# Gated FNet and PEER mix on one core: operand sums moved into DRAM transfers, row transposes moved to DMA

## The chip, the cores and the metric

The kernel runs on one core of a Trainium2 chip. The metric is device time in microseconds (us), the median of several runs. Five engines work side by side, each on its own list of instructions in order: TensorE (PE) multiplies matrices, VectorE (DVE), ScalarE (ACT) and GpSimd (POOL) work on elements, and SyncE (SP) mostly issues DMA transfers. ACT and POOL can issue transfers too. An instruction that waits holds up all that stands behind it on its engine.

## The reference

The input x has 2048 rows of 640 numbers. Two branches are computed from it and mixed row by row with a gate.

```python
g = sigmoid((x * gate_w).sum(-1))
# branch A: a Fourier transform over both axes, real part, as matrix products
a = einsum("sd,ed->se", x, dft_hid_re);  b = einsum("sd,ed->se", x, dft_hid_im)
y = dft_seq_re @ a - dft_seq_im @ b
# branch B: 32 heads; each scores 16 + 16 keys and takes the best two of each,
# then the best two of the four sums (of 256 experts); softmax over those two
act = gelu(einsum("nd,nhkd->nhk", x, u[top_e]))
o = einsum("nhk,nhk,nhkd->nd", softmax(top_s), act, v[top_e])
return g * y + (1 - g) * o
```

## The kernel before

Every matrix product in float32 is made of three products: each operand is split into a high part (an ACT copy to fp32r) and a low part (a subtraction on POOL or DVE); `split` does that and `mm3` issues the three matmuls. `mm3` and `split` are helpers, so nearly all matmuls carry the lines L127 to L129 and all splits L122 (ACT) and L123 (POOL or DVE).

**First stage, 128 pieces.** `seq_piece(n)` multiplies x by one 128 x 512 block of the sequence transform: two matrices (`w`), four column blocks of 512 (`c`), 16 pieces each, 15 matmuls in a piece. Piece n loads the block of piece n + 5 (tile `wf`, five buffers, on SP's queue) and splits that of piece n + 3 into one of the four slots of `WS`. After the 16 pieces of a block its five sums are evicted to `ST`, multiplied by the gate on DVE (`gate_piece`, L192) and stored to DRAM as `pd[w, c]` (`store_piece`, L201, issued by ACT).

What else is to be done is hung behind pieces: `at(n, f)` puts f into the program behind piece n. Up to piece 31 the key matrix is prepared, from piece 31 to 71 (`N0` to `N1`) score products for branch B are put between the pieces, from 71 on the hidden transform's matrices are loaded and split (`load_dd`, `split_dd`, tiles with the tags `xf`, `xh`, `xl`).

**The pump.** DVE's work for branch B is a list of small steps that `Pump` puts into the program between PE's matmuls. Each matmul group adds its time to a credit (times `share`: 0.95, or 1.05 while the experts run), each step takes its cost off, and other DVE work takes off its own (`bg.credit -= ...`). `topk` picks the best keys of a tile of 128 rows, `gates` makes the weights of four tiles, and `rows` turns the results so that heads lie on partitions: six PE transposes in one group for two tiles into a PSUM bank, two ACT copies (L501) from there into `ROWS`. `bg.space(f, us)` calls f when that much matmul time has gone by since the step before it.

When all 16 tiles have rows, `experts` starts: 32 chunks (2 halves of 16). For each, DVE builds one-hot tiles (`hot`, three operations, cost 3.3), PE multiplies them (16 matmuls, L593), DVE sums the result into `cd` (L579, L581, cost 1.4). From piece 120 on (`ending`) there is one chunk at a time.

**Second stage, 70 steps.** The hidden transform is done on blocks of 2 x 2 with seven products in place of eight, for two pairs `b` of column blocks, 35 steps each (`step(m)`). The operands are four blocks of the pair (`a11`, `a12`, `a21`, `a22`, that is `pd[0]` and `pd[1]` of the pair's two columns) or sums of them:

- s3 = a21 + a11, s1 = a21 + a22, s2 = s1 + a11, s4 = s2 + a12.

The order of the products is a11, a12, s1, s2, s4, s3, a22, five steps each. `load_a` loads an operand block of 256 KB on SP's queue into a buffer given out by `take` and given back by `give`; `split_step` splits it five steps ahead. The sums come about in two ways. For the pair b = 0, `load_parts` loads the blocks behind pieces 95 to 106, `sum_parts` adds them on DVE and `store_parts` stores the four sums to DRAM (`pq`). For b = 1, blocks are loaded again and added in place on DVE at steps 39 to 52 (`add_a`).

At the start of each half, `load_z` brings in the branch B operands: it drains the pump until the half's sums `cd` are issued, stores them (`gd`, L549), loads them back (L806) with the activations (`actd`) and the gate, and `split_z` multiplies them on DVE (L819, L820) and splits them into `zo`.

Of the kernel before, what the change touches and what calls it, by code (L numbers as in the profile page):

```python
# [8 lines left out]
F32 = mybir.dt.float32  # L9
F32R = mybir.dt.float32r  # L10
F16 = mybir.dt.float16
AF = mybir.ActivationFunctionType
OP = mybir.AluOpType
# [3 lines left out]
P = 128  # L17
# [7 lines left out]
NT = S // P  # L25
NP = NT // 2
TC = 512
NC = S // TC
NPC = 2 * NC * NT
KD = D // P  # L30
HALF = D // 2
NG = HH // 8
NB = 4
# [57 lines left out]
def gated_mix_kernel(ctx: ExitStack, tc: tile.TileContext, xT, xn, dreT, dimT, wsre, wsim, wq, kT, uT, vv, gw, out):  # L91
    nc = tc.nc
# [3 lines left out]
    big = ctx.enter_context(tc.tile_pool(name="big", bufs=1))  # L96
    dram = ctx.enter_context(tc.tile_pool(name="dram", bufs=1, space=bass.MemoryType.DRAM))
# [8 lines left out]
    def bank(n, shape=(P, TC), dt=F32):  # L106
        return psum.tile(list(shape), dt, name=f"b{n}", tag=f"b{n}")
# [4 lines left out]
    def ps_t(shape, dt=F32):  # L112
        return bank(7, shape, dt)
# [6 lines left out]
    def split(f, h, l, eng):  # L120

        nc.scalar.activation(h, f, AF.Copy)  # L122
        eng.tensor_sub(l, f, h.bitcast(F32))  # L123
# [5 lines left out]
        nc.tensor.matmul(o, wl, ah, start=False, stop=last, skip_group_check=more)  # L129

    pd = {(w, c): dram.tile([KD, P, TC], F32, name=f"pd{w}{c}", tag=f"pd{w}{c}") for w in range(2) for c in range(NC)}
    pq = {u: dram.tile([KD, P, TC], F32, name=f"pq{u}", tag=f"pq{u}") for u in ("s1", "s2", "s4", "s3")}
    actd = dram.tile([2, P, S], F32, name="actd")
    gd = [dram.tile([2, 4, E, E, P], F32, name=f"gd{g}", tag=f"gd{g}") for g in range(2)]
    gdr = dram.tile([S], F32, name="gdr")
    bg = Pump()
# [16 lines left out]
    pf, psp, X, xr = {}, {}, {}, {}  # L153
# [17 lines left out]
    def at(n, f, *args):  # L171
        then.setdefault(n, []).append(lambda: f(*args))
# [5 lines left out]

    banks = []
    p3, last_part, ending, share = None, False, False, 0.95  # L180
    grow, staged, P22 = {}, {}, {}

    def load_row(q):
        grow[q] = pools[-1].tile([P, TC], F32, name="grow", tag="grow")
# [10 lines left out]

    def store_piece(q):
        w, c = divmod(q, NC)
        if q == NC + 1:
            P22.update((d, staged[q, d]) for d in range(KD))
        for d in range(KD):  # L200
            nc.scalar.dma_start(pd[w, c][d], staged.pop((q, d)))  # L201

# [20 lines left out]
    for q in range(2 * NC):  # L223
        n = NT * (q + 1)
        at(n + (2 if q == 0 else -2 if q > 1 else -1), load_row, q)
        at(n + (7 if q == 0 else 0), gate_piece, q)
        at(n + (8 if q == 0 else 1), store_piece, q)
# [47 lines left out]
    t = ps_t([P, 512])  # L275
# [18 lines left out]
    ident = const.tile([P, P], F16)  # L294
# [52 lines left out]
    xf, xs = {}, {}  # L347
# [25 lines left out]
    n = bursts[-1]  # L373
# [28 lines left out]
    ROWS = [cp.tile([P, 3, P, 8], F16, name=f"rows{g}") for g in range(2)]  # L402
    p2_stack = ctx.enter_context(ExitStack())
    p2 = p2_stack.enter_context(tc.tile_pool(name="p2", bufs=1, reuse_waits="tile"))
# [5 lines left out]
    picked, rowed = set(), set()  # L410
# [79 lines left out]
    def rows(b):  # L490
        rp, gs = gated.pop(b)

        def row_tiles(a):
            t = ps_t([P, 2, 3, P], F16)
            for m in range(2):
                for n in range(2):
                    nc.tensor.transpose(t[:, m, n, :], rp[:, n, a + m].rearrange("p a k h -> p (a k h)"), ident)  # L497
                nc.tensor.transpose(t[:, m, 2, :], gs[:, a + m].rearrange("p a k h -> p (a k h)"), ident)
            for m in range(2):
                i = b * NB + a + m  # L500
                nc.scalar.activation(ROWS[i // 8][:, :, :, i % 8], t[:, m], AF.Copy)  # L501
                rowed.add(i)

        for a in range(0, NB, 2):
            bg.space(lambda a=a: row_tiles(a), 7.0 if a else 20.0 if b == NT // NB - 1 else 12.0)
        yield 0.0

    def done(i, gen):
# [3 lines left out]
    def picks(i, sc):  # L512
        bg.add(done(i, topk(i, sc)))
        if i % NB == NB - 1:
            bg.add(gates(i // NB))
        elif i and i % NB == 0:
            bg.add(rows(i // NB - 1))
        if i == NT - 1:
            bg.add(rows(NT // NB - 1))
# [14 lines left out]
    for p in range(NP):  # L534
        n = N0 + 5 * p
# [4 lines left out]
    N1 = N0 + 5 * NP  # L540
# [174 lines left out]
    at(NPC + 28, store_gates, 1)  # L715


    raw_free, raw_tags = deque(), [("wf", 1)] * 5 + [(f"X{s}", 2) for s in range(10, 16)] + [("xf", 2)]
    raw, sp = {}, {}

    def take(key):
        if raw_tags:
            t, n = raw_tags.pop(0)
            if t == "wf":
                raw_free.append(big.tile([P, TC], F32, name="ra", tag=t, bufs=5))
            else:
                r = big.tile([P, 2, TC], F32, name="ra", tag=t)
                raw_free.extend(r[:, a] for a in range(2))
        raw[key] = f = raw_free.popleft()
        return f  # L730

    def give(key):
        raw_free.append(raw.pop(key))

    def load_a(b, what, k, row, col):
        f = take((b, what, k))
        nc.sync.dma_start(f, pd[col - 1, 2 * b + row - 1][k] if row else pq[what][k])

    def add_a(b, o, what, k, last):
        nc.vector.tensor_add(raw[b, o, k], raw[b, o, k], raw[b, what, k])  # L740
        bg.credit -= 0.75
        if last:
            give((b, what, k))


    PS, parts = [], {}

    def load_parts(k):

        if not PS:  # L750
            PS.extend(big.tile([P, 2, TC], F32, name="ps", tag=t) for t in ("xf", "xh", "xl"))
        parts[k] = [t[:, k % 2] for t in PS]
        for f, q in zip(parts[k], ((0, 1), (0, 0), (1, 0))):
            nc.sync.dma_start(f, pd[q][k])

    def sum_parts(k, n):
        f21, f11, f12 = parts[k]
        f22 = P22[k]
        if n == 0:
            nc.vector.tensor_add(f22, f22, f21)  # L760
            nc.vector.tensor_add(f21, f21, f11)
        else:
            nc.vector.tensor_add(f11, f11, f22)
            nc.vector.tensor_add(f12, f12, f11)
        bg.credit -= 1.5

    def store_parts(k, n):
        f21, f11, f12 = parts[k]
        for u, f in (("s2", f11), ("s4", f12)) if n else (("s1", P22[k]), ("s3", f21)):
            nc.sync.dma_start(pq[u][k], f)  # L770

    for k, (n, m) in enumerate(((-1, 2), (0, 4), (5, 7), (7, 9), (10, 12))):
        n, m = NT * (NC + 2) + n, NT * (NC + 2) + m
        at(n, load_parts, k)
        for a in range(2):
            at(m + a, sum_parts, k, a)
            at(m + 2 + a, store_parts, k, a)

    def ring(m):
        return WP[:, m % 6] if m % 6 < 2 else WS[:, m % 6 - 2]  # L780

    def split_step(m):
        if m < 2 * NSTEP:
            b, (u, k) = m // NSTEP, divmod(m % NSTEP, KD)
            what = UNITS[u]
            key = (b, "s" if b and what in ("s1", "s2", "s4") else what, k)
            sp[m] = ring(m)[:, 0], ring(m)[:, 1]
            split(raw[key], *sp[m], nc.vector if what in ("s2", "s3") else nc.gpsimd)
            bg.credit -= 0.8 if what in ("s2", "s3") else 0.0
            if b == 0 or what in ("a11", "a12", "a22", "s3", "s4"):  # L790
                give(key)

    zop = {}

    def load_z(b, n):

        c = 2 * b + n
        bg.drain(lambda: b in summed)
        store_gates(b)
        nc.sync.dma_start(take((b, "g", n)), gdr[c * TC:(c + 1) * TC].partition_broadcast(P))  # L800
        for k in range(2):
            a, f = take((b, "za", k)), take((b, "zf", k))
            nc.sync.dma_start(a, actd[k][:, c * TC:(c + 1) * TC])
            for i in range(4):
                i8 = (4 * c + i) % 8
                nc.sync.dma_start(f[:, i * P:(i + 1) * P],  # L806
                                  gd[b][i8 // 4, i8 % 4].rearrange("e f m -> (e f) m")[k * P:(k + 1) * P])
# [74 lines left out]
    def step(m):  # L882
        b, (u, k) = m // NSTEP, divmod(m % NSTEP, KD)
        what = UNITS[u]
        if k == 0:
# [8 lines left out]
            if what == "a22":  # L894
                z_group("Z", 0, v_neg, first=True)
        split_step(m + AHEAD)
        o, w, w5 = {
            "a11": ("X", lambda a: DD[:, 0, a, k, 0:2 * P], lambda a: DD[:, 0, a, k, 4 * P:]),
# [51 lines left out]
    M = NPC  # L950
# [8 lines left out]
    M = NPC + NSTEP  # L959
    for k in range(KD):  # L960
        at(M - 8 + k, load_a, 1, "a11", k, 1, 1)
        at(M - 4 + k, load_a, 1, "a12", k, 1, 2)
        at(M + k, load_a, 1, "s", k, 2, 2)
        at(M + k, load_a, 1, "s3", k, 2, 1)
        at(M + 4 + k, add_a, 1, "s", "s3", k, False)
        at(M + 5 + k, load_a, 1, "a11", k, 1, 1)
        at(M + 8 + k, add_a, 1, "s", "a11", k, False)
        at(M + 8 + k, add_a, 1, "s3", "a11", k, True)
        at(M + 8 + k, load_a, 1, "a12", k, 1, 2)
        at(M + 13 + k, add_a, 1, "s", "a12", k, True)  # L970
        at(M + 21 + k, load_a, 1, "a22", k, 2, 2)
    for b in range(2):
        M = NPC + b * NSTEP
        for n, i in ((0, -1), (1, 21)):
# [76 lines left out]
```

## Time and profile before

| | |
|---|---|
| three runs | 787.89, 788.63, 789.27 us; median 788.63 |
| the profiled execution | 788.78 us, its span 787.0 us |
| busy share of the span | PE 99%, weight loads 79%, DVE 70%, POOL 43%, ACT 35% |
| matmuls | 4164 |
| DMA | 128.73 MB, mean 164 GB/s |
| granted PE clock | 0.998 |

The profile is of one execution. The span runs from the first to the last instruction on the core. In a row of groups, the number behind x is the count, then come the busy time and the mean of one in ns, then the idle time of the engine just before them and what ended it. In a timeline row, the start and the length in us stand first. In a row of waits: in total, how often, the longest. Matmuls are pipelined and their ends are modelled, so the pace is read from start to start.

### The profile page before, as it was taken

How to read it: one execution, taken by the hardware profiler on the slowest of the kernel's cores; microseconds unless marked ns; L12 is line 12 of the kernel's file. 1: busy time of each engine (PE TensorE's matmuls, PEld its weight loads, DVE VectorE, ACT ScalarE, POOL GpSimd, SP SyncE). 2: the span in 40 equal slices, each digit the busy share in tenths (PEclk: the TensorE clock that was granted, in tenths of full speed). 3: DMA queues.
4: the chain of work that ended last, by engine and by line, in shares of the span. 5: the costliest groups of instructions: out<-in, count | busy, mean ns of one | idle time of the engine just before them, and what ended most of it. 6: DMA issues, size and time to landing. Idle time of an engine off the chain costs nothing.

```text
span 787.0 us, 11023 instructions
## 1 busy us (share of the span) xinstructions
PE 777.9 (99%) x4164; PEld 625.3 (79%) x4164; DVE 550.5 (70%) x660; ACT 274.3 (35%) x445; POOL 335.1 (43%) x233
## 2 busy tenths in 40 slices
PE   9999999999999999999999999999999999998997
PEld 6777677888888888888888888888888877777886
DVE  6741022286887799499969598899989947673861
ACT  5344323321316332532353551311334344323350
POOL 5423224315334241533415784444346573355370
PEclk9999999999999999999999999999999999999999
DMA  9966995403022230305213533578855795329621
GB/s 347 370 246 189 322 342 183 166 13 101 20 96 86 108 114 14 100 14 186 77 60 121 189 121 104 164 234 266 266 167 172 255 314 173 108 64 305 216 84 67
DMA packets 67828, 128.73 MB, mean 164 GB/s; under 512 B 9408, under 2 KB 16448, under 8 KB 67520
## 3 DMA queue, kind: packets, MB, share of 16 engines
q1 hardware_dynamic: 55024, 110.60, 42.2%
q10 hardware_dynamic: 12752, 17.45, 6.2%
q8 instruction: 32, 0.52, 0.3%
q14 instruction: 20, 0.16, 0.1%
HBM read 102.84 MB, written 25.17 MB: 163 GB/s over the span
## 4 chain that ended last, share of the span: by engine, by line
PE 92%; DMA 3%; POOL 1%; issue 1%; SPq 1%; ACT 1%; DVE 0%; ACTq 0%; DVEq 0%; POOLq 0%
PE b L127 30%; PE b L128 29%; PE b L129 29%; PE b L320 2%; DMA ra<-pqs 1%; PE b L593 1%; DMA ra<-actd 1%; POOL WS L123 1%; PE b L332 1%; PE b L213 1%; POOL zo L123 1%; DMA ra<-gd 0%; DMA wf<-in_wsre 0%; SPq L806 0%; PE b L497 0%
## 5 line engine op out<-in xcount | busy, mean ns | idle before, releaser
L123 POOL TENSOR_TENSOR WS<-wf,WS 128x512 fp32r<-128x512 f32 x127 | 190.0, 1502 | 272.7 <-ACT WS L122 254.8
L127 PE MATMUL b<-WS,X 128*128 128x512 f32 x635 | 251.3, 396 | 0.1
L129 PE MATMUL b<-WS,X 128*128 128x512 f32 x635 | 247.6, 390 | 0.0
L128 PE MATMUL b<-WS,X 128*128 128x512 f32 x635 | 247.5, 390 | 0.0
L127 PEld LDWEIGHTS b<-WS,X 128*128 128x128 f32 x635 | 119.2, 188 | 32.8 <-issue 7.8
L129 PEld LDWEIGHTS b<-WS,X 128*128 128x128 f32 x635 | 119.2, 188 | 25.4
L128 PEld LDWEIGHTS b<-WS,X 128*128 128x128 f32 x635 | 119.3, 188 | 24.0 <-POOL WS L123 0.4
L122 ACT ACTIVATE WS<-wf 128x512 fp32r<-128x512 f32 x128 | 80.1, 629 | 128.5 <-PE b L129 75.5
L437 DVE TENSOR_REDUCE mm<-sc 128x64 f32<-128x1024 f32 x32 | 39.0, 1219 | 45.2 <-ACT sc L423 44.7
L123 POOL TENSOR_TENSOR xl<-xf,xh 128x640 fp32r<-128x640 f32 x16 | 33.0, 2086 | 73.4 <-ACT xh L122 73.4
L127 PE MATMUL b<-WU,xh 128*128 128x512 f32 x160 | 62.7, 392 | 0.0
L129 PE MATMUL b<-WU,xl 128*128 128x512 f32 x160 | 62.3, 389 | 0.0
L128 PE MATMUL b<-WU,xh 128*128 128x512 f32 x160 | 62.3, 389 | 0.0
L423 ACT ACTIVATE sc<-b 128x512 f32<-128x512 f32 x32 | 20.5, 641 | 114.4 <-PE b L129 114.4
L123 POOL TENSOR_TENSOR WS<-ra,WS 128x512 fp32r<-128x512 f32 x32 | 45.6, 1444 | 27.8 <-ACT WS L122 27.8
L192 DVE SCALAR_TENSOR_TENSOR ST<-ST,grow 128x512 f32<-128x512 f32 x40 | 35.7, 956 | 18.3 <-DMA grow<-gdr 18.3
L335 DVE TENSOR_TENSOR WU<-b,WU 128x512 fp32r<-128x512 f32 (+1 forms) x16 | 7.8, 490 | 57.3 <-ACT WU L334 57.3
L439 DVE TENSOR_TENSOR eq<-sc,mm 128x1024 f16<-128x1024 f32 x32 | 45.5, 1423 | 1.1
L579 DVE TENSOR_TENSOR tmp<-b,mask 128x512 f32<-128x512 f32 x32 | 22.0, 689 | 30.4 <-PE b L593 29.3
L443 DVE TENSOR_REDUCE rr<-eq 128x64 f16<-128x1024 f16 x32 | 39.0, 1220 | 1.1
L123 POOL TENSOR_TENSOR WP<-ra,WP 128x512 fp32r<-128x512 f32 x18 | 26.8, 1498 | 29.5 <-ACT WP L122 29.4
L122 ACT ACTIVATE WS<-ra 128x512 fp32r<-128x512 f32 x46 | 28.0, 627 | 25.5 <-PE b L129 14.4
(152 smaller groups left out, 1258.1 us busy)
## 6 DMA issues: line engine op xcount, KB each, us to landing
wq<-in_wq SPq DMA_DIRECT2D x32, 640.0 KB, 6.5
wf<-in_wsre SPq DMA_DIRECT2D x64, 256.0 KB, 5.5
wf<-in_wsim SPq DMA_DIRECT2D x64, 256.0 KB, 3.8
ra<-pd SPq DMA_DIRECT2D x50, 256.0 KB, 4.1
pd<-ST ACTq DMA_DIRECT2D x40, 256.0 KB, 3.0
xr<-in_xn SPq DMA_DIRECT2D x16, 320.0 KB, 5.9
xf<-in_xT SPq DMA_DIRECT2D x16, 320.0 KB, 3.3
ra<-pqs SPq DMA_DIRECT2D x20, 256.0 KB, 4.3
```

The costliest lines, as they stand in the source:

```text
L122: nc.scalar.activation(h, f, AF.Copy)
L123: eng.tensor_sub(l, f, h.bitcast(F32))
L127: nc.tensor.matmul(o, wh, ah, start=first, stop=False, skip_group_check=more)
L128: nc.tensor.matmul(o, wh, al, start=False, stop=False, skip_group_check=more)
L129: nc.tensor.matmul(o, wl, ah, start=False, stop=last, skip_group_check=more)
L192: nc.vector.scalar_tensor_tensor(f, f, -1.0 if w else 1.0, g, op0=OP.mult, op1=OP.mult)
L320: nc.tensor.matmul(ps[32 * j:32 * j + 32, :HALF], kp[:, 8 * G // H, r, :], w[:, j], start=(r == 0), stop=(r == 1))
L423: nc.scalar.activation(scs[i].rearrange("p h e -> p (h e)")[:, c], ps, AF.Copy)
L437: nc.vector.tensor_reduce(m, sc, op=OP.max, axis=AX.X)
L439: nc.vector.tensor_tensor(eq, sc, m[:, :, None].to_broadcast([P, HH, E]), op=OP.is_equal)
L443: nc.vector.tensor_reduce(r, eq, op=OP.max, axis=AX.X)
L579: nc.vector.tensor_tensor(tmp, t.rearrange("p m (e t) -> p (m e) t", t=4), mask4[:, None, :].to_broadcast([P, 8 * E, 4]), op=OP.mult)
```

## The change

1. The operand sums of both pairs are made in DRAM. `pq` now has four sums for each pair. `copy_sum` copies a whole block set of 1.25 MB from DRAM to DRAM on SP's queue; `add_sum` adds another onto it with two accumulating transfers issued by POOL, of three and two blocks of 256 KB. `pair_sums` puts them behind pieces: for b = 0 copies behind 75, 79, 81 and 83, sums behind 77, 84, 100, 102 and 104; for b = 1 copies behind 91, 95, 97 and 99, sums behind 93 and 116 and behind steps 5, 10 and 15. `load_parts`, `sum_parts`, `store_parts` and `add_a` are gone, and both pairs load their sums with `load_a`.
2. `take` gives out buffers that were never used in the second stage first, then those given back. Before, both stood in one queue.
3. The row transposes are DMA transposes issued on SP's queue, three for a tile, into the tile `rt` (two buffers), and ACT copies from there. A tile's transposes and the copy of the tile before it are one step; steps are 5 us of matmul time apart, and the first comes after 8 us (16 for the last four tiles) instead of 12 (20).

```diff
@@ -129,7 +129,8 @@
         nc.tensor.matmul(o, wl, ah, start=False, stop=last, skip_group_check=more)
 
     pd = {(w, c): dram.tile([KD, P, TC], F32, name=f"pd{w}{c}", tag=f"pd{w}{c}") for w in range(2) for c in range(NC)}
-    pq = {u: dram.tile([KD, P, TC], F32, name=f"pq{u}", tag=f"pq{u}") for u in ("s1", "s2", "s4", "s3")}
+    pq = {(b, u): dram.tile([KD, P, TC], F32, name=f"pq{b}{u}", tag=f"pq{b}{u}")
+          for b in range(2) for u in ("s1", "s2", "s4", "s3")}
     actd = dram.tile([2, P, S], F32, name="actd")
     gd = [dram.tile([2, 4, E, E, P], F32, name=f"gd{g}", tag=f"gd{g}") for g in range(2)]
     gdr = dram.tile([S], F32, name="gdr")
@@ -178,7 +179,7 @@
 
     banks = []
     p3, last_part, ending, share = None, False, False, 0.95
-    grow, staged, P22 = {}, {}, {}
+    grow, staged = {}, {}
 
     def load_row(q):
         grow[q] = pools[-1].tile([P, TC], F32, name="grow", tag="grow")
@@ -195,8 +196,6 @@
 
     def store_piece(q):
         w, c = divmod(q, NC)
-        if q == NC + 1:
-            P22.update((d, staged[q, d]) for d in range(KD))
         for d in range(KD):
             nc.scalar.dma_start(pd[w, c][d], staged.pop((q, d)))
 
@@ -490,19 +489,29 @@
     def rows(b):
         rp, gs = gated.pop(b)
 
-        def row_tiles(a):
-            t = ps_t([P, 2, 3, P], F16)
-            for m in range(2):
-                for n in range(2):
-                    nc.tensor.transpose(t[:, m, n, :], rp[:, n, a + m].rearrange("p a k h -> p (a k h)"), ident)
-                nc.tensor.transpose(t[:, m, 2, :], gs[:, a + m].rearrange("p a k h -> p (a k h)"), ident)
-            for m in range(2):
-                i = b * NB + a + m
-                nc.scalar.activation(ROWS[i // 8][:, :, :, i % 8], t[:, m], AF.Copy)
-                rowed.add(i)
-
-        for a in range(0, NB, 2):
-            bg.space(lambda a=a: row_tiles(a), 7.0 if a else 20.0 if b == NT // NB - 1 else 12.0)
+        def load_rows(a):
+
+            t = p2.tile([P, 3, P], F16, name="rt", bufs=2)
+            for n in range(3):
+                f = rp[:, n, a] if n < 2 else gs[:, a]
+                nc.sync.dma_start(t[:, n, :], f.rearrange("p a k h -> p (a k h)"), transpose=True)
+            return t
+
+        def put_rows(a, t):
+            i = b * NB + a
+            nc.scalar.activation(ROWS[i // 8][:, :, :, i % 8], t, AF.Copy)
+            rowed.add(i)
+
+        got = {}
+
+        def step(a):
+            if a < NB:
+                got[a] = load_rows(a)
+            if a:
+                put_rows(a - 1, got.pop(a - 1))
+
+        for a in range(NB + 1):
+            bg.space(lambda a=a: step(a), 5.0 if a else 16.0 if b == NT // NB - 1 else 8.0)
         yield 0.0
 
     def done(i, gen):
@@ -715,18 +724,18 @@
     at(NPC + 28, store_gates, 1)
 
 
-    raw_free, raw_tags = deque(), [("wf", 1)] * 5 + [(f"X{s}", 2) for s in range(10, 16)] + [("xf", 2)]
+    fresh, raw_free, raw_tags = deque(), deque(), [("wf", 1)] * 5 + [(f"X{s}", 2) for s in range(10, 16)] + [("xf", 2)]
     raw, sp = {}, {}
 
     def take(key):
-        if raw_tags:
+        if not fresh and raw_tags:
             t, n = raw_tags.pop(0)
             if t == "wf":
-                raw_free.append(big.tile([P, TC], F32, name="ra", tag=t, bufs=5))
+                fresh.append(big.tile([P, TC], F32, name="ra", tag=t, bufs=5))
             else:
                 r = big.tile([P, 2, TC], F32, name="ra", tag=t)
-                raw_free.extend(r[:, a] for a in range(2))
-        raw[key] = f = raw_free.popleft()
+                fresh.extend(r[:, a] for a in range(2))
+        raw[key] = f = (fresh or raw_free).popleft()
         return f
 
     def give(key):
@@ -734,47 +743,32 @@
 
     def load_a(b, what, k, row, col):
         f = take((b, what, k))
-        nc.sync.dma_start(f, pd[col - 1, 2 * b + row - 1][k] if row else pq[what][k])
-
-    def add_a(b, o, what, k, last):
-        nc.vector.tensor_add(raw[b, o, k], raw[b, o, k], raw[b, what, k])
-        bg.credit -= 0.75
-        if last:
-            give((b, what, k))
-
-
-    PS, parts = [], {}
-
-    def load_parts(k):
-
-        if not PS:
-            PS.extend(big.tile([P, 2, TC], F32, name="ps", tag=t) for t in ("xf", "xh", "xl"))
-        parts[k] = [t[:, k % 2] for t in PS]
-        for f, q in zip(parts[k], ((0, 1), (0, 0), (1, 0))):
-            nc.sync.dma_start(f, pd[q][k])
-
-    def sum_parts(k, n):
-        f21, f11, f12 = parts[k]
-        f22 = P22[k]
-        if n == 0:
-            nc.vector.tensor_add(f22, f22, f21)
-            nc.vector.tensor_add(f21, f21, f11)
-        else:
-            nc.vector.tensor_add(f11, f11, f22)
-            nc.vector.tensor_add(f12, f12, f11)
-        bg.credit -= 1.5
-
-    def store_parts(k, n):
-        f21, f11, f12 = parts[k]
-        for u, f in (("s2", f11), ("s4", f12)) if n else (("s1", P22[k]), ("s3", f21)):
-            nc.sync.dma_start(pq[u][k], f)
-
-    for k, (n, m) in enumerate(((-1, 2), (0, 4), (5, 7), (7, 9), (10, 12))):
-        n, m = NT * (NC + 2) + n, NT * (NC + 2) + m
-        at(n, load_parts, k)
-        for a in range(2):
-            at(m + a, sum_parts, k, a)
-            at(m + 2 + a, store_parts, k, a)
+        nc.sync.dma_start(f, pd[col - 1, 2 * b + row - 1][k] if row else pq[b, what][k])
+
+
+    def flat(t):
+        return t.rearrange("k p t -> (k p) t")
+
+    def copy_sum(b, u, src):
+        nc.sync.dma_start(flat(pq[b, u]), flat(src))
+
+    def add_sum(b, u, w, row):
+        for r in (slice(0, 3), slice(3, KD)):
+            nc.gpsimd.dma_start(flat(pq[b, u][r]), flat(pd[w, 2 * b + row][r]), accum_op=OP.add, max_dma_last_dim=2048)
+
+    def pair_sums(b, n0, n1, n2, gap):
+
+        at(n0, copy_sum, b, "s3", pd[0, 2 * b + 1])
+        at(n0 + 2, add_sum, b, "s3", 0, 0)
+        at(n0 + 4, copy_sum, b, "s1", pd[0, 2 * b + 1])
+        at(n0 + 6, copy_sum, b, "s2", pq[b, "s3"])
+        at(n0 + 8, copy_sum, b, "s4", pq[b, "s3"])
+        at(n1, add_sum, b, "s4", 1, 0)
+        for i, u in enumerate(("s1", "s2", "s4")):
+            at(n2 + gap * i, add_sum, b, u, 1, 1)
+
+    pair_sums(0, N1 + 4, NT * (NC + 1) + 4, NT * (NC + 2) + 4, 2)
+    pair_sums(1, N1 + 20, NT * (NC + 3) + 4, NPC + 5, 5)
 
     def ring(m):
         return WP[:, m % 6] if m % 6 < 2 else WS[:, m % 6 - 2]
@@ -783,12 +777,11 @@
         if m < 2 * NSTEP:
             b, (u, k) = m // NSTEP, divmod(m % NSTEP, KD)
             what = UNITS[u]
-            key = (b, "s" if b and what in ("s1", "s2", "s4") else what, k)
+            key = (b, what, k)
             sp[m] = ring(m)[:, 0], ring(m)[:, 1]
             split(raw[key], *sp[m], nc.vector if what in ("s2", "s3") else nc.gpsimd)
             bg.credit -= 0.8 if what in ("s2", "s3") else 0.0
-            if b == 0 or what in ("a11", "a12", "a22", "s3", "s4"):
-                give(key)
+            give(key)
 
     zop = {}
 
@@ -960,15 +953,11 @@
     for k in range(KD):
         at(M - 8 + k, load_a, 1, "a11", k, 1, 1)
         at(M - 4 + k, load_a, 1, "a12", k, 1, 2)
-        at(M + k, load_a, 1, "s", k, 2, 2)
-        at(M + k, load_a, 1, "s3", k, 2, 1)
-        at(M + 4 + k, add_a, 1, "s", "s3", k, False)
-        at(M + 5 + k, load_a, 1, "a11", k, 1, 1)
-        at(M + 8 + k, add_a, 1, "s", "a11", k, False)
-        at(M + 8 + k, add_a, 1, "s3", "a11", k, True)
-        at(M + 8 + k, load_a, 1, "a12", k, 1, 2)
-        at(M + 13 + k, add_a, 1, "s", "a12", k, True)
-        at(M + 21 + k, load_a, 1, "a22", k, 2, 2)
+        at(M + k, load_a, 1, "s1", k, 0, 0)
+        at(M + 4 + k, load_a, 1, "s2", k, 0, 0)
+        at(M + 8 + k, load_a, 1, "s4", k, 0, 0)
+        at(M + 13 + k, load_a, 1, "s3", k, 0, 0)
+        at(M + 19 + k, load_a, 1, "a22", k, 2, 2)
     for b in range(2):
         M = NPC + b * NSTEP
         for n, i in ((0, -1), (1, 21)):
```

## The prediction

> **What bounds the kernel now.** I read the busy shares first, then what TensorE (PE) waited for, then PE's own timeline wherever the next matmul started late.
>
> ```profile
> span 787.0 us, 11023 instructions
> PE 777.9 (99%) x4164; PEld 625.3 (79%) x4164; DVE 550.5 (70%) x660; ACT 274.3 (35%) x445; POOL 335.1 (43%) x233
> PE b L128 <- POOL WS L123: 2.6, 2, 2.0
> PE b L128 <- POOL WP L123: 0.9, 1, 0.9
> ```
>
> PE is busy for 99% of the span and its few waits are for POOL's half of a split. So only two things can shorten the time: PE instructions that go, and places where PE stands. The worst such place, in PE's timeline:
>
> ```profile
> 722.29 0.50 PE L127 MATMUL b<-WS,DD 128*128 128x512 f32 x1
> 724.80 0.50 PE L128 MATMUL b<-WS,DD 128*128 128x512 f32 x1 [2.01 <-POOL WS L123]
> 729.68 0.40 PE L127 MATMUL b<-zo,vxh 128*128 128x512 f32 x1
> ```
>
> From 722.29 to 729.68 there are 15 matmul starts in 7.39 us. The usual pace is shown by POOL's splits, one for each piece of 15 matmuls:
>
> ```profile
> 467.42 6.85 POOL L123 TENSOR_TENSOR WS<-wf,WS 128x512 fp32r<-128x512 f32 x4
> 476.39 1.29 POOL L123 TENSOR_TENSOR WS<-wf,WS 128x512 fp32r<-128x512 f32 x1 [2.12 <-ACT WS L122]
> 479.80 1.38 POOL L123 TENSOR_TENSOR WS<-wf,WS 128x512 fp32r<-128x512 f32 x1 [2.12 <-ACT WS L122]
> ```
>
> 479.80 - 476.39 = 3.41 us for 15, or 0.227 each. The stop costs 7.39 - 3.41 = 4.0 us: 2.3 of standing, the rest in slow matmuls behind it. What came late is seen in the timelines of SP, DVE and PE, and in the chain that ended last (the two short POOL rows):
>
> ```profile
> 695.82 0.44 PE L593 MATMUL b<-hot 128*64 128x64 f16 x16
> 701.86 0.44 PE L593 MATMUL b<-hot 128*64 128x64 f16 x16
> 703.13 0.44 PE L593 MATMUL b<-hot 128*64 128x64 f16 x16
> 704.59 0.69 DVE L581 TENSOR_REDUCE cd<-tmp 128x128 f32<-128x512 f32 x1
> SPq L549 <- DVE cd L581: 30.8, 1, 30.8
> 705.30 1.17 SPq L549 DMA_DIRECT2D gd<-cd  x2
> 714.04 2.17 SPq L806 DMA_DIRECT2D ra<-gd  x4
> 718.68 1.65 DVE L819 TENSOR_TENSOR ra<-ra 128x512 f32<-128x512 f32 x1 [0.93 <-DMA ra<-gd]
> 721.80 1.28 POOL zo L123
> 723.07 1.68 POOL WS L123
> ```
>
> The last expert chunk's sum ends at 705.3. SP, held 30.8 us for it, stores the gate sums, reads them back, DVE multiplies, POOL splits zo, and only behind that the WS tile that PE needs. The last two chunks came 1.3 us apart (the one before, 6 us earlier): load_z drained the pump there. The chain starts when the pump ends.
>
> **Transposes.** In PE's timeline one group of six costs:
>
> ```profile
> 250.10 0.39 PE L129 MATMUL b<-WU,xl 128*128 128x512 f32 x1
> 250.33 0.29 PE L497 MATMUL b<-ident,rp 128*128 128x128 f16 x2
> 250.65 0.48 PE L127 MATMUL b<-WU,xh 128*128 128x512 f32 x1
> 250.97 0.39 PE L128 MATMUL b<-WU,xh 128*128 128x512 f32 x1
> L497 PE MATMUL b<-ident,rp 128*128 128x128 f16 x32 | 3.6, 222 | 0.0
> L498 PE MATMUL b<-ident,gs 128*128 128x128 f16 x16 | 3.1, 219 | 0.0
> ```
>
> From 250.33 to 250.97 is 0.64 us, of which one matmul would have taken 0.23; so 0.41. The 48 transposes make eight groups: **-3.3 us**, all of it on PE's path. In their place SP issues 48 transposing DMAs of 32 KB, whose landing no row shows. The evictions stay:
>
> ```profile
> L501 ACT ACTIVATE rows<-b 128x384 f16<-128x384 f16 x16 | 29.3, 2094 | 17.0 <-PE b L498 17.0
> ra<-gd SPq DMA_DIRECT2D x32, 64.0 KB, 2.7
> ra<-pd SPq DMA_DIRECT2D x50, 256.0 KB, 4.1
> pd<-ST ACTq DMA_DIRECT2D x40, 256.0 KB, 3.0
> q1 hardware_dynamic: 55024, 110.60, 42.2%
> ```
>
> A row buffer comes free at the eviction of two tiles before, and its new tile is evicted two steps of 5 us later; less 2.1 us for the eviction that leaves 7.9 us for three transposes. Overlapped they land like the 64 KB row, 2.7 us; one after the other, 8.1. I take the first and zero cost; ends 0 and 16 x 0.2 = +3 us. If that cover is gone, ACT stands, with PSUM evictions and splits queued behind it. SP may wait for the gates on DVE before a first transpose; behind it wait the wf loads, which five buffers and three finished splits cover for some 10 us. Below nothing is excluded, since PE's share is already counted.
>
> **DVE adds and the pump.** The adds that go, from the groups by line:
>
> ```profile
> L760 DVE TENSOR_TENSOR ST<-ST,ps 128x512 f32<-128x512 f32 x5 | 5.8, 1154 | 0.0
> L761 DVE TENSOR_TENSOR ps<-ps 128x512 f32<-128x512 f32 x5 | 5.3, 1069 | 0.2
> L764 DVE TENSOR_TENSOR ps<-ps 128x512 f32<-128x512 f32 x5 | 4.5, 892 | 0.2
> L763 DVE TENSOR_TENSOR ps<-ps,ST 128x512 f32<-128x512 f32 x5 | 4.4, 879 | 0.1
> L740 DVE TENSOR_TENSOR ra<-ra 128x512 f32<-128x512 f32 x20 | 15.8, 830 | 3.7 <-DMA ra<-pd 2.4 <-POOL WS L123 1.2
> ```
>
> 36 us of DVE work, none on PE's path by itself. What counts is the credit: sum_parts took 5 x 2 x 1.5 = 15 us out of the pump before the second stage, and the change gives it back. The rows take some: the last ones are finished 16 + 4 x 5 = 36 us after their start and not 20 + 7 = 27, so experts start 9 us later, at share 1.05 9.5 us of credit. Net +5.5, and a chunk is 3.3 + 1.4 = 4.7: the experts run one chunk ahead. The drain at load_z goes, and the last burst, 703.13 now, stands about 4 us earlier against PE's other work (a chunk further by the 6 us between the first two bursts, less what the credit adds up to by then). The gate chain moves with it: WS comes at about 720.7 where PE asks at 722.3. **-4.0 us**; ends 0 (the chain stays) and -5 (a little also of the 0.9 us wait for WP). Late next is POOL, with four splits behind zo. The L740 adds lie behind the stop and delayed no matmul: 0.
>
> **Copies and accumulating transfers.** The 15 part loads and 20 part stores go, and eight copies of 1.25 MB (as much as 40 such transfers) and ten sums come, each two transfers on POOL's queue: three and two blocks. SP's copies of "s3" wait for the sum that fills it; behind them stand wf loads, rows and draws. I take 0 (the sum is issued four pieces, 13.6 us, ahead); ends 0 and +2 for each of two pairs. Bytes: DMA is busy less than half of the time; 0.
>
> POOL is where it is decided. No row shows how long POOL is held by issuing a transfer; call it G for the two transfers of a sum. Lower end: like an SP issue, 0.32 to 0.6 us each (1.17 for the two gd stores), G = 1. Upper end: POOL stands until the transfers land. One packet takes 0.422 x 16 x 787.0 / 55024 = 0.097 us; the first transfer has 384 rows on 16 engines, 24 each, read from two places: 48 x 0.097 = 4.6 us, plus the fixed part of a 256 KB store (3.0 less its eight packets, 0.8) 2.2: 6.8. The second 3.1 + 2.2 = 5.3. So G = 12.
>
> Against that stand POOL's reserves. A split is made three pieces ahead. The sums at n = 100, 102, 104: POOL is free 0.7 + 1.4 us into piece 100, the next split is asked 4 x 3.41 us after the start and takes 1.5, so 10 us; with the expert bursts 10.6. Two pieces give back 6.8 - 3.0 = 3.8. PE stands for 3G - 7.6 - 10.6, from G = 6.1 on. At n = 84 the four splits at 467.42 run back to back (pieces 87 to 90), the second ends at 470.8 and piece 88 starts at 475.7: 4.9 us. Counted in the same way, m = 5 leaves 5.7 us (POOL is late there already) and m = 15 4.8; n = 77, 93, 116 about 8 to 10; m = 10 more, as DVE splits s2. I take G = 4, nearer to the issue row, since the engine has nothing to do with the bytes: cost 0. If the cover is gone, G = 8 costs 3.1 + 5.8 + 2.3 + 3.2 = 14.4, and slow matmuls after the stops, at most 1.7 each as at 724.80, some 3 more.
>
> **Unused buffers first.** a11's fourth load no longer waits for a buffer that split 0 gives back; s1's third waits for xf until V is split. Both lie 10 us and more ahead of their splits: 0.
>
> **The sum**, against the profiled execution's 788.78 us (span 787.0 and 1.8 around it; 0.15 above the median of 788.63): 788.78 - 3.3 - 4.0 = **781.5 us**.
>
> **The rivals.** *POOL is held until the first transfer of each pair has landed* (other side): G = 6.8 + 1.2 = 8, 781.5 + 17 = 798 us; it decides from G = 6.8 on, where the loss reaches 7.3. For it: two transfers directly one behind the other, ten times, on the engine PE already waits for. Against it: 9 us of reserve at most places. Chance 0.27. [...]
>
> *DVE starves POOL's issuing.* The eq and hot operations swing with POOL's splits beside them:
>
> ```profile
> L571 DVE TENSOR_TENSOR hot<-rows,wtab x32: 676/684/2067, 454.3 to 699.0; 128x1024 f16<-128x1024 f16 x32
> ```
>
> At worst three times as long; G = 4 x 3 = 12 gives 7.1 + 17.8 + 6.3 + 7.2 = 38 us, 820. But the median is undisturbed: 0.06. [...]
>
> *Transposes land late:* 10 us for three means 16 x 2.1 = 34 us, 815. 0.09.
>
> *The gate chain stays:* only the transposes are gained, 785.3. 0.08.
>
> *It cancels out* (G near 6.8, or SP's waits eat it): 788. 0.08.
>
> **How the numbers follow.** 0.42 is left for the forecast, its own range 779 to 784 (the ends of the terms). Below 779 lies 0.05; above 802, where G passes 8.5 or the dear rivals lie, 0.15. So 779 to 802. Within 0.2% (1.6 us) a measurement can't be told from no change. Faster: 0.42 + 0.08 = 0.50; same 0.08; slower 0.27 + 0.06 + 0.09 = 0.42.
>
> **What would show it.** Right: no L497 rows, 4116 matmuls; the gap at 722 gone; last L593 burst followed by a gate store with PE 4 us further back; POOL's rows without holes after the sums. Wrong: PE waits for POOL's WS at pieces 88, 106, 108 and in the steps after m = 5 and 15, with POOL idle ahead of its splits; ACT's rows waiting for DMA.

## The result, and the profile after

The changed kernel took 844.3 us (median of 5 runs, 841.24 to 847.03), the kernel before 788.59 in the same comparison: ratio 1.0705, 95% interval 1.0685 to 1.0724. It is slower by 56 us, where 781.5 was forecast. The page of the changed kernel, taken in an execution of 847.0 us, with the chain that ended last:

```profile
span 845.2 us, 10951 instructions
PE 789.7 (93%) x4116; PEld 633.3 (75%) x4116; DVE 498.7 (59%) x620; ACT 274.9 (33%) x445; POOL 340.7 (40%) x253
PE   9999999999999999999995889978979969499997
PE 68%; issue 13%; DMA 7%; POOL 6%; DVE 4%; SPq 1%; ACT 1%; POOLq 0%; DVEq 0%; ACTq 0%
```

The 48 transposes are gone (4116 matmuls) and DVE has 52 us less to do, but PE's share fell from 99% to 93%, all of it in the second half of the span. "issue" now holds 13% of the chain. The waits say whose:

```profile
PE b L128 <- POOL WS L123: 44.4, 11, 10.8
PE b L127 <- ACT WS L122: 1.5, 1, 1.5
...
POOL pq0s L757 <- issue: 40.7, 7, 11.1
POOL pq1s L757 <- issue: 38.3, 5, 10.2
POOL pq1s L757 <- DMA ra<-gd: 13.4, 1, 13.4
```

PE waited 44.4 us for POOL's half of a split (2.6 before), and POOL itself stood about 79 us at L757, the accumulating transfers, and 13.4 more that the profile puts down to a load. In POOL's timeline:

```profile
440.56 1.15 POOL L757 DMA_DIRECT2D pq0s<-pd  x1 [2.99 <-DMA pq0s<-pd]
452.76 0.90 POOL L757 DMA_DIRECT2D pq0s<-pd  x1 [11.05 <-issue]
481.45 0.92 POOL L757 DMA_DIRECT2D pq0s<-pd  x1
488.80 0.89 POOL L757 DMA_DIRECT2D pq0s<-pd  x1 [6.43 <-issue]
489.38 4.05 POOL L123 TENSOR_TENSOR WS<-wf,WS 128x512 fp32r<-128x512 f32 x3
714.99 0.88 POOL L757 DMA_DIRECT2D pq1s<-pd  x1 [13.44 <-DMA ra<-gd]
```

Writing out one transfer takes 0.88 to 1.15 us. But between the first and the second of a sum POOL stands 6 to 13 us, and the splits that PE needs stand behind the second. PE's timeline at the first sum, and the windows around it (behind the length: busy time of PE, weight loads, DVE, ACT and POOL with the instructions, then the granted clock, the share of the DMA engines, GB/s; a packet's whole time is counted where it starts, so a share can pass 1):

```profile
447.16 0.39 PE L127 MATMUL b<-WS,X 128*128 128x512 f32 x1
456.89 0.80 PE L128 MATMUL b<-WS,X 128*128 128x512 f32 x1 [9.34 <-POOL WS L123]
457.48 0.63 PE L129 MATMUL b<-WS,X 128*128 128x512 f32 x1
457.91 0.63 PE L127 MATMUL b<-WS,X 128*128 128x512 f32 x1
460.33 0.40 PE L127 MATMUL b<-WS,X 128*128 128x512 f32 x1
```

```profile
445.00:450.00 5.00, 2.55 (x12) 1.77 (x10) 4.70 (x8) 2.58 (x5) 0.00 (x0) 0.99 1.23 289
450.00:455.00 5.00, 0.00 (x0) 0.00 (x0) 5.00 (x9) 1.91 (x1) 2.24 (x2) 0.50 0.62 236
455.00:460.00 5.00, 3.11 (x7) 2.49 (x8) 0.71 (x2) 0.00 (x0) 5.00 (x4) 0.50 0.79 163
```

This stop is paid twice: 9.5 us of standing, then matmuls that start 0.43 us apart and not 0.227, at a granted clock of 0.50, until 460.33.

For each pair of neighbouring matmul starts more than 0.26 us apart, I added up what is over 0.227: 20.2 us before, 80.5 after. Of the 60.3 us that came in, the stops named below make 47.2, a wait of the expert matmuls for DVE ahead of 633.86 makes 2.7, and slow matmuls behind the stops some 12; the stop of 2.3 us at 722.29 went. G is read as the prediction has it, from the first issue of a sum to POOL's next work.

| sum behind | first issue at (us) | G (us) | PE stops (us) |
|---|---|---|---|
| piece 77 | 440.56 | 12.8 | 9.5 |
| 84 | 481.45 | 7.9 | 3.2 |
| 93 | 512.51 | 10.3 | 0 |
| 100, 102, 104 | 543.21, 556.01, 569.19 | 7.8, 8.1, 7.5 | 1.3, 5.2, 3.2 |
| 116 | 613.80 | 11.0 | 3.0 |
| steps 5, 10, 15 | 683.61, 700.60, 720.80 | 11.7, 15.0, 7.8 | 5.6, 1.3, 11.1 |
| (ScalarE, then POOL, at 471.70) | | | 3.7 |

How long the new transfers take from issue to landing (KB each, median us):

```profile
pq0s<-pd POOLq DMA_DIRECT2D x5, 768.0 KB, 7.1
pq1s<-pd POOLq DMA_DIRECT2D x5, 768.0 KB, 10.1
pq0s<-pd POOLq DMA_DIRECT2D x5, 512.0 KB, 5.4
rt<-rp SPq DMA_TRANSPOSE x32, 3.3
rt<-gs SPq DMA_TRANSPOSE x16, 2.4
```

G goes with the landing of the first transfer, 7.1 and 10.1 us in the median. It does so one by one: in all ten sums the second transfer is issued 0.26 us after the first has landed (481.45 and 7.1 for the landing make 488.5; the second starts at 488.80). That holds for 714.99 too, where the profile names a load. The theory to be tested: the scratch that the kernel sets aside for such transfers, 1024 bytes (`dynamic_dma_scratch_size`; descriptor queue or ring in the expectations), has no room for the second until the first is through.

### The profile page after: what moved, and what is told of

It is laid out like the page before. It is cut to its first block, busy times and chain, and to the rows that moved or that the text cites. A ratio compares the mean times of both kernels' runs of the same rounds, so it can differ in the third digit from the quotient of the medians.

```text
span 845.2 us, 10951 instructions
## 1 busy us (share of the span) xinstructions
PE 789.7 (93%) x4116; PEld 633.3 (75%) x4116; DVE 498.7 (59%) x620; ACT 274.9 (33%) x445; POOL 340.7 (40%) x253
## 4 chain that ended last, share of the span: by engine, by line
PE 68%; issue 13%; DMA 7%; POOL 6%; DVE 4%; SPq 1%; ACT 1%; POOLq 0%; DVEq 0%; ACTq 0%
PE b L127 22%; PE b L128 21%; PE b L129 21%; POOL WS L123 4%; DMA pd<-ST 3%; PE b L319 2%; DMA wf<-in_wsim 2%; DMA pq0s<-pd 1%; DVE ST L193 1%; POOL pq1s L757 1%; DMA ra<-gd 1%; POOL pq0s L757 1%; SPq L497 1%; PE b L331 1%; DVE tf L687 1%
## 5 line engine op out<-in xcount | busy, mean ns | idle before, releaser
L123 POOL TENSOR_TENSOR WS<-wf,WS 128x512 fp32r<-128x512 f32 x127 | 185.8, 1501 | 246.7 <-ACT WS L122 241.9
L128 PE MATMUL b<-WS,X 128*128 128x512 f32 x635 | 253.3, 399 | 26.4 <-POOL WS L123 26.4
L127 PE MATMUL b<-WS,X 128*128 128x512 f32 x635 | 255.6, 402 | 1.5 <-ACT WS L122 1.5
L129 PE MATMUL b<-WS,X 128*128 128x512 f32 x635 | 251.9, 397 | 0.0
L128 PEld LDWEIGHTS b<-WS,X 128*128 128x128 f32 x635 | 122.1, 192 | 53.3 <-POOL WS L123 29.2
L127 PEld LDWEIGHTS b<-WS,X 128*128 128x128 f32 x635 | 121.8, 192 | 35.9 <-issue 7.8
L129 PEld LDWEIGHTS b<-WS,X 128*128 128x128 f32 x635 | 122.1, 192 | 26.0
L122 ACT ACTIVATE WS<-wf 128x512 fp32r<-128x512 f32 x128 | 80.5, 630 | 150.0 <-PE b L129 86.3
L123 POOL TENSOR_TENSOR WS<-ra,WS 128x512 fp32r<-128x512 f32 x32 | 43.6, 1401 | 17.5 <-ACT WS L122 17.5
L193 DVE SCALAR_TENSOR_TENSOR ST<-ST,grow 128x512 f32<-128x512 f32 x40 | 31.6, 853 | 17.7 <-ACT ST L219 10.4
L128 PE MATMUL b<-WS,DD 128*128 128x512 f32 x72 | 29.3, 407 | 12.6 <-POOL WS L123 12.6
L502 ACT ACTIVATE rows<-rt 128x384 f16<-128x384 f16 x16 | 30.9, 1962 | 27.6 <-DMA rt<-gs 27.6
```

The source lines that it names most:

```text
L127: nc.tensor.matmul(o, wh, ah, start=first, stop=False, skip_group_check=more)
L128: nc.tensor.matmul(o, wh, al, start=False, stop=False, skip_group_check=more)
L193: nc.vector.scalar_tensor_tensor(f, f, -1.0 if w else 1.0, g, op0=OP.mult, op1=OP.mult)
L502: nc.scalar.activation(ROWS[i // 8][:, :, :, i % 8], t, AF.Copy)
```

## Experiments

Times are medians; the kernel before ran beside each (788.41 to 788.96).

| kernel | us | ratio, 95% interval |
|---|---|---|
| e1, scratch of 2048 bytes | 798.56 | 1.0124 (1.0109 to 1.0139) |
| e9, of 1536 bytes | 797.98 | 1.0121 (1.0103 to 1.0138) |
| e2, the two transfers of a sum apart | 788.92 | 1.0002 (0.9982 to 1.0022) |
| e3, row transposes alone | 791.16 | 1.0032 (1.0021 to 1.0043) |
| e4, sums and buffer order alone | 837.22 | 1.0621 (1.0590 to 1.0653) |
| e6, e2 with PE transposes | 785.22 | 0.9958 (0.9944 to 0.9972) |
| e5, e2 with early copies | 781.97 | 0.9913 (0.9899 to 0.9927) |
| e7, e5 with 2048 bytes | 782.09 | 0.9914 (0.9900 to 0.9927) |
| e10, e1 with early copies | 785.47 | 0.9957 (0.9944 to 0.9971) |
| e8, e5 with the old buffer order | 782.76 | 0.9917 (0.9904 to 0.9931) |

**e1: a larger scratch.** Three small tiles moved to another pool to make room.

```diff
-    nc = bacc.Bacc("TRN2", target_bir_lowering=False, num_devices=1, dynamic_dma_scratch_size=1024)
+    nc = bacc.Bacc("TRN2", target_bir_lowering=False, num_devices=1, dynamic_dma_scratch_size=2048)
```

> The changed kernel with 2048 bytes in place of 1024 for POOL's descriptor queue (identity and key tiles moved to the first pool to make room); nothing else differs. Theory (POOL is held because the second transfer of a sum finds no room in the queue until the first has landed): the issue rows stay at 0.9 us, the 6 to 11 us holes between the two of a pair go, PE's stops at the pieces behind the sums and in steps 11 to 21 go, and the time is 782 to 787 us. Rival 1 (the accumulating transfers and copies slow the loads and splits by their traffic): the stops stay within a few us, 830 us or more. Rival 2 (DVE keeps POOL from writing descriptors): the issue rows and holes stay, 840 us.

POOL's timeline at the sum behind piece 84 and at step 10, then ScalarE's and PE's at the one large stop that is left:

```profile
477.50 1.86 POOL L757 DMA_DIRECT2D pq0s<-pd  x2
478.69 3.22 POOL L123 TENSOR_TENSOR WS<-wf,WS 128x512 fp32r<-128x512 f32 x2
666.09 1.87 POOL L757 DMA_DIRECT2D pq1s<-pd  x2 [4.18 <-issue]
...
456.41 11.86 ACTq L200 DMA_DIRECT2D pd<-ST  x5
468.31 0.74 ACT L122 ACTIVATE DD<-draw 128x640 fp32r<-128x640 f32 x1 [14.18 <-issue]
...
461.55 0.39 PE L129 MATMUL b<-WS,X 128*128 128x512 f32 x1
469.62 0.79 PE L127 MATMUL b<-WS,X 128*128 128x512 f32 x1 [7.68 <-ACT WS L122]
```

The two transfers now go out back to back in 1.86 us and the splits follow at once: 45.7 of the 55.7 us came back with one number. The bytes to be moved and DVE's work are the same as in the change, so neither made the holes. POOL still waits where sums follow closely. The rest is a stop of 10 us at 461.55, where ScalarE took 11.9 us to issue five stores and PE waited for its split. That second cause was not in the expectation, which the time missed by some 12 us.

**e9: how much room.** The same with 1536 bytes.

> The changed kernel with a scratch of 1536 bytes for GpSimd's descriptors (1024 in the change, 2048 gave 798.6 us). [...] If the wait ends only when the queue is empty, or the first transfer must have landed whatever the size short of some larger step, the holes stay as with 1024: 835 to 845 us.

```profile
440.90 2.07 POOL L757 DMA_DIRECT2D pq0s<-pd  x2 [3.08 <-DMA pq0s<-pd]
477.13 1.85 POOL L757 DMA_DIRECT2D pq0s<-pd  x2
540.02 0.95 POOL L757 DMA_DIRECT2D pq0s<-pd  x1 [2.50 <-issue]
543.20 0.90 POOL L757 DMA_DIRECT2D pq0s<-pd  x1 [2.23 <-issue]
```

With 1536 bytes the two transfers of a sum go out back to back again, in 1.85 to 2.07 us at pieces 77 and 84, where with 1024 POOL stood 6 to 13 us between them: the case in which the holes stay, 835 to 845 us, is out. Only sums that come closely behind another still stand, and both of their transfers do: 2.5 and 2.2 us here, 4.1 and 3.8 at step 10. The room, and no other thing about the transfers, is what held POOL. How much of it a transfer takes no row shows. By these runs a sum needs more than 1024 bytes and at most 1536. In e1 a sum and the first transfer of the next need more than 2048, since that transfer still stands until the first of the sum before has landed (if the need goes with the blocks, five of eight here, a sum takes over 1280, an estimate):

```profile
540.06 1.88 POOL L757 DMA_DIRECT2D pq0s<-pd  x2 [1.92 <-issue]
```

**e2: the transfers apart.** The scratch of 1024 bytes, the two transfers of a sum three to six pieces or steps from each other, copies put to suit.

```diff
-    def add_sum(b, u, w, row):
-        for r in (slice(0, 3), slice(3, KD)):
-            nc.gpsimd.dma_start(...)
+    def add_part(b, u, w, row, part):
+        r = (slice(0, 3), slice(3, KD))[part]
+        nc.gpsimd.dma_start(...)
...
+    add_parts(0, "s3", 0, 0, 77, 80)
+    add_parts(0, "s4", 1, 0, 86, 89)
```

> The changed kernel, queue of 1024 bytes, the same 20 accumulating transfers and 8 copies, but the two transfers of a sum three or more pieces (five or more steps) apart, so that the first has landed before the second is issued. Theory of the full queue: no holes but where a landing takes more than 10 us, 782 to 790 us. Rival 1 (traffic): bytes are the same, so 830 us or more. Rival 2 (DVE): issues are as many, so 840 us.

It gave 788.92 us (786.80 to 793.33), no different from before. POOL's stops no longer reach PE. One stop is left, of 4.0 us at 462.69, with slow matmuls to 471.4; ScalarE's stores in front of it:

```profile
452.07 11.41 ACTq L200 DMA_DIRECT2D pd<-ST  x5
463.53 0.74 ACT L122 ACTIVATE DD<-draw 128x640 fp32r<-128x640 f32 x1 [9.51 <-DMA pd<-ST]
```

**e3 and e4: each part alone.** e3 is the kernel before with only the row transposes by DMA; e4 is the changed kernel with PE's transposes put back.

> The kernel before with the DMA transposes alone; sums as before on DVE. By the pump's credit the experts start 9 us later and get nothing back, so load_z drains four chunks at step 34 where it drained two: the gate store comes some 6 us later than in the kernel before, PE's stop near 722 grows from 4 to about 10 us, PE saves 3.3 us: 788.6 - 3.3 + 6 = 791 us (788 to 796). Rival (the transposes land too late, ACT stands and PE with it): stops before 450 us in the profile, 800 us or more. Rival (the transposes cost nothing and the pump is not what sets the stop): 785 us.

> The changed kernel with the PE transposes of before and 1024 bytes of queue. If the DMA transposes add nothing to the holds: 844 + 3 = 847 us, with the same holes. If part of the loss is theirs (the hole of 11 us behind piece 77 and the ACT stores that took 19 us fall among them): 825 to 840 us, the hole behind piece 77 near 7 us and the ACT stores in under 6 us.

e4 has 837.22 us: nearly the whole loss is that of the sums, and the transposes add 7.1 us to it. The time fell into the range of the second case, its signs did not: the hole behind piece 77 is 13.5 us, not 7, and ScalarE's stores take 17.5 us, not under 6. So neither is made by the transposes:

```profile
457.56 0.90 POOL L747 DMA_DIRECT2D pq0s<-pd  x1 [13.51 <-DMA pd<-ST]
454.57 17.53 ACTq L200 DMA_DIRECT2D pd<-ST  x4
```

e3 is slower than before by 2.2 us although PE has 48 instructions less. Its PE waits:

```profile
PE b L603 <- DVE tmp L589: 5.4, 3, 2.7
PE b L127 <- ACT ST L937: 1.6, 1, 1.6
```

The expert chunks end later and are drained in front of load_z with PE waiting for DVE. The time came out as expected, but as several stops of up to 2.7 us and not as one of 10 us near 722. So the DMA transposes alone did not pay here; that they pay where the DVE time that the sums set free pulls the pump forward is an estimate, which no run shows by itself.

**e6: which part makes the stop at 462.** e2 with PE's transposes.

> The kernel with the parts apart, with the rows transposed by TensorE as before the change (+3.3 us of TensorE). Theory 'copies and sums alone fill the DMA engines': ScalarE's stores at 452 us are still held over 10 us, the stop at 462 us stays, 788.9 + 3.3 = 792 us. Rival 'it takes the 48 transposes as well to make TensorE stop': the stop of 4 us and the slow matmuls behind it go, 788.9 + 3.3 - 6 = 786 us.

785.22 us, near the rival's 786, but neither theory holds as put: ScalarE's last three stores are still held 8.5 us, and a stop of 2.1 us stays where e2 has 4.0. Copies and sums alone delay the stores; the transposes add to it. In e2 they cost about 3.7 us net (e2's interval is 1.6 us to each side), that is some 7 against the 3.3 that they save by the prediction's reading.

**e5 and e7: the copies moved out of the crowd.** The three copies and the sum that ran at 434 to 460 us are issued behind pieces 66 to 72, where their operands have long been stored, the next two copies behind piece 88, and the next two sums change places; e7 has 2048 bytes too.

```diff
-    at(75, copy_sum, 0, "s3", pd[0, 1])
-    add_parts(0, "s3", 0, 0, 77, 80)
-    at(79, copy_sum, 0, "s1", pd[0, 1])
-    at(84, copy_sum, 0, "s2", pq[0, "s3"])
-    at(84, copy_sum, 0, "s4", pq[0, "s3"])
-    add_parts(0, "s4", 1, 0, 86, 89)
-    at(82, copy_sum, 1, "s3", pd[0, 3])
-    add_parts(1, "s3", 0, 0, 92, 95)
+    at(66, copy_sum, 0, "s3", pd[0, 1])
+    at(69, copy_sum, 0, "s1", pd[0, 1])
+    add_parts(0, "s3", 0, 0, 69, 72)
+    at(72, copy_sum, 1, "s3", pd[0, 3])
+    at(88, copy_sum, 0, "s2", pq[0, "s3"])
+    at(88, copy_sum, 0, "s4", pq[0, "s3"])
+    add_parts(1, "s3", 0, 0, 86, 89)
+    add_parts(0, "s4", 1, 0, 92, 95)
```

> From the kernel with the parts apart (788.9 us): three of the copies that ran at 434 to 460 us (s3 and s1 of pair 0, s3 of pair 1) and the first accumulating transfers are issued at step 66 to 72 (about 375 to 415 us), and the two copies of pair 0 that follow at step 88, after the last row transposes. The score loop and ScalarE's stores at 452 to 463 us then no longer meet the copies. Theory 'the transfers of 435 to 470 us fill the DMA engines' (DMA share 0.95 to 1.24 there, against 0.15 to 0.68 before the change): the five stores at 452 us are issued in under 5 us instead of 11.4, the stop of TensorE at 462 to 471 us (1.9 + 2.1 us and some 10 matmuls at 0.43 instead of 0.23) goes, 783 us (781 to 785). Rival 'the DMA transposes themselves hold the stores': the stop stays, 788 to 790 us.

> The early copies of e5 and the 2048-byte scratch of e1 together. If full queue and crowded transfers are all there is, GpSimd's holes that are left with the parts apart (3 to 7 us, four or five) go too; they hold no matmul there, so the time is that of e5 within 1 us, 783 us. If something else on GpSimd is late, such as the wait for the copy to land, the time goes below e5 by up to 2 us or not at all.

781.97 and 782.09 us: the best of the kernels, and the time forecast for the change. Room for POOL adds nothing once the transfers are apart. The window from 455 to 460 us in the kernel before, e1 and e5:

```profile
455.00:460.00 5.00, 5.00 (x28) 4.00 (x27) 5.00 (x3) 4.22 (x7) 5.00 (x3) 1.00 0.39 134
```

```profile
455.00:460.00 5.00, 5.00 (x24) 4.14 (x23) 4.96 (x9) 0.00 (x0) 0.00 (x0) 1.00 1.20 319
```

```profile
455.00:460.00 5.00, 5.00 (x23) 4.13 (x22) 5.00 (x5) 4.68 (x6) 3.86 (x3) 1.00 0.79 257
```

The DMA engines were busy for 0.39 of it before, over 1 in e1, where ScalarE did nothing at all, and 0.79 in e5. ScalarE's stores and POOL's longest hold in e5's timeline, then its PE waits:

```profile
451.62 3.66 ACTq L200 DMA_DIRECT2D pd<-ST  x4
487.40 0.89 POOL L757 DMA_DIRECT2D pq1s<-pd  x1 [10.41 <-issue]
```

```profile
PE b L128 <- POOL WP L123: 0.9, 1, 0.9
PE b L128 <- POOL WS L123: 0.8, 2, 0.6
```

The stores go out in 3.7 us and the stop is gone. A hold of POOL of 10.4 us is still there, and one matmul behind it, at 489.66, starts 0.2 us late: with one transfer at a time the splits just keep their lead.

**e10: only the two causes taken away.** e1 with the copies where e5 has them, and the sums in one go; sums for the pieces 77, 84 and 93 stand behind 69, 92 and 86.

```diff
-    at(n0 + 2, add_sum, b, "s3", 0, 0)
...
+    at(69, add_sum, 0, "s3", 0, 0)
...
+    at(86, add_sum, 1, "s3", 0, 0)
+    at(92, add_sum, 0, "s4", 1, 0)
```

> The changed kernel with 2048 bytes and with only the copies and two sums moved out of the crowded 40 us (three copies to step 66 to 72, two to step 88, one sum to 69, 86 and 92); both transfers of every sum are issued one behind the other as in the change. If the two causes (ring too small for a sum, and transfers crowding at 435 to 470 us) make up the whole loss, 782.5 us (781.5 to 784). If a sum issued in one go holds GpSimd even with the larger ring where three follow within 4 steps, 785 to 790 us.

785.47 us, the second case, 3.5 us over e5. POOL is held 4.1 and 4.5 us at steps 10 and 15. The profiled executions are 2.2 us apart (784.47 and 782.24), and late matmul starts, counted as above, make 2.1 of it (18.1 us against 16.0): PE has four short stops of 0.3 to 0.5 us that e5 lacks (1.7 us in all) and one of 1.0 us where expert matmuls wait for DVE, and lacks some of e5's. Why the median of e10 lies 1.0 us over its profiled execution stays open.

**e8: the order of buffers taken back** to that before the change, in e5.

```diff
-        raw[key] = f = (fresh or raw_free).popleft()
+        raw[key] = f = raw_free.popleft()
...
```

> The kernel with the early copies (782.0 us), with the order of operand buffers taken back to that before the change (a new buffer is made at every request, the oldest free one is handed out). The prediction gave this part 0. If that holds: 782 us (781.2 to 782.8). Rival 'the buffers that free late hold SyncE's loads': SyncE waits at the fourth load of a11 and of s1, the loads behind come late, and the second stage loses 2 to 6 us: 784 to 788.

782.76 us (781.48 to 783.00) against e5's 781.97 (781.63 to 782.76): not to be told apart. In e8's profile POOL's hold at 488 us is 11.5 us, 1.1 more than in e5, and PE stands 1.3 us behind it, so the lead of the splits is nearly used up there.

## Why the prediction was wrong, step by step

**The step that failed** is "I take G = 4, nearer to the issue row, since the engine has nothing to do with the bytes". G was 7.5 to 15.0, 10.0 in the mean. The engine does have to do with the bytes: with 1024 bytes of scratch it didn't issue the second transfer before the first had landed, in any of the ten sums. The rival that said so stood in the text with 0.27. That the size of the scratch decides it, e1 and e9 show; no row of before does.

**Most reserves were right, the rival's price was not.** With the measured G the prediction's own formulas give 7.9 - 4.9 = 3.0 us at piece 84 (measured 3.2), 11.7 - 5.7 = 6.0 at step 5 (5.6), and 23.4 + 2.8 - 18.2 = 8.0 at pieces 100 to 104 (9.7; the 2.8 is POOL's wait for a store ahead of the sum). At piece 77 it doesn't come out: a reserve of 8 to 10 against a G of 12.8 and 3.0 us of waiting for the copy leaves 6 to 8, and PE stood 9.5. Three things made 63 us (844.3 - 781.5) of the rival's 17. First, G = 8 was worked out for transfers that have the DMA engines nearly to themselves; in five of the ten sums the first one landed only after 9.4 to 14.1 us, beside other transfers, of which no row shows the one that slows it. So pieces 77 and 116, which the rival had covered, cost 9.5 and 3.0 us. Second, a sum waits for the second transfer of the sum before it too (2.2 and 2.3 us at 102 and 104, 3.6 at step 15), and step 10 was held 15 us, so that step 15 met a POOL already late: 11.1 us where 3.0 came out. Third, behind each stop of 3 us or more come slow matmuls, five to eleven of them starting 0.42 or 0.43 us behind the one before, some 12 us in all and not 3. From 456.89 to 460.33 they last 3.4 us; the clock granted from 455 to 460 us is 0.50.

**Bytes "less than half of the time; 0".** This was a mean over the span. In the 35 us from 435 on, where copies, a sum, row transposes, matrix loads and stores meet, the share is 0.5 to 1.2 in windows of 5 us (0.15 to 0.68 before), and ScalarE's stores take 19 us to be issued, 11 to 13 in e1, e2 and e9. It cost 3.7 us here, hidden in part behind POOL's stops, and 10 us and slow matmuls in e1. SP's copies were given ends of 0 and 2; the loss fell on an engine that the prediction did not look at.

**Transposes.** Budget and landing were right: 3.3 and 2.4 us (2.7 estimated), and though ACT stood 27.6 us in nine waits for them, which the prediction had among the signs of being wrong, no matmul was held by it before 447 us. "Zero cost" held in e5, not in e2, where they crowd the same stretch. No run isolates the -3.3 itself.

**The gate chain** was right: the stop at 722 is gone. In e5 the last gate sums are stored at 698.45, not 705.30, and no matmul behind 640 us starts more than 0.3 us late:

```profile
698.45 1.17 SPq L558 DMA_DIRECT2D gd<-cd  x2
713.04 1.29 POOL L123 TENSOR_TENSOR zo<-ra,zo 128x512 fp32r<-128x512 f32 x1 [3.55 <-ACT zo L122]
721.51 0.39 PE L127 MATMUL b<-zo,vxh 128*128 128x512 f32 x1
```

At that store PE has started 2719 of its 128x512 matmuls, 2738 before: 19 times 0.227 us make 4.3 us further back, where 4 was forecast. The last two expert bursts are still 2 us apart there (694.56 and 696.53), so they came earlier rather than further apart. e3, where the credit of the sums is missing and the time goes up by 2.2 us, and e6, where the store comes at matmul 2635 with that credit and PE's transposes, fit that the credit did it; no run parts the credit from the DVE time that the sums set free. **Unused buffers first** was put at 0: e8 agrees.

**DVE starves POOL's issuing** (0.06) is out: an issue took 0.90 us at 452.76 in a window where DVE was busy 5.00 of 5.00 us, and 0.92 at 481.45, where DVE did nothing; and in e1 the holes go with DVE's work unchanged.

## What to carry to other kernels

A transfer that GpSimd issues is not free once it is issued: with 1024 bytes of scratch the engine stood 7.5 to 15.0 us over a sum, until its first transfer had landed, and everything behind it in its list stood too; with 1536 a sum alone went out in about 2 us. Look at that size before pairing such transfers, then either give them room or put several splits between them. And read the DMA share at the place where new transfers land, not over the span: moving a few copies and sums into a quieter stretch was worth 7 us here (e2 to e5), as much as the whole gain that was forecast.

## What was not expected of the hardware

Half as much scratch again (1536 for 1024 bytes) was worth 46 us here. Stores of 256 KB from ScalarE, five of which took 11 to 19 us to issue from 452 to 457 us on against 3.7 for four in e5, stood on the issuing engine. The DMA share was 0.5 to 1.3 meanwhile, and lowest where they stood longest, so it alone doesn't say what holds them; which limit does, no row shows. Accumulating 768 KB from DRAM onto DRAM took 6.6 to 14.1 us in the changed kernel (medians 7.1 and 10.1).
